# Transposing DMAs of gathered rows moved from ScalarE's queue to SyncE's, with a fourth buffer, new planned times, and expert 0's rows taken block by block

## The chip, the cores and the metric

The kernel runs on one core of one Trainium2 chip, as one launch. The metric is the device time of that launch in microseconds, the median of several executions. Profiles are of one execution; times in them are counted from the start of its span. Engines are named as the profile does: PE (TensorE), DVE (VectorE), ACT (ScalarE), POOL (GpSimd), SP (SyncE). A DMA is issued by an instruction on an engine's queue (SPq, ACTq, POOLq) and its data moves afterwards on the core's 16 DMA engines.

## The reference, cut to what matters

Three stages follow each other: a gated linear attention over 4 sequences, 8 heads, 768 steps, head size 48; a mixture of 8 experts, in which each of 3072 tokens goes to one expert; a second feed-forward layer over all tokens.

```python
# stage 1: state = alpha * state + k v^T ; y = q state
x = attn_out.transpose(0, 2, 1, 3).reshape(B * S, H * D)          # 3072 x 384
# stage 2
logits = unit(x) @ unit(expert_emb).T / tau
expert_idx = argmax(logits, axis=1)                                # one expert a token
for e in range(8):
    mask = expert_idx == e
    h = np.maximum(x[mask] @ w1[e], 0.0)                           # 384 -> 1024
    out[mask] = gate_w[mask, None] * (h @ w2[e])                   # 1024 -> 384
# stage 3
h = x @ w_in                                                       # 384 -> 2048
return np.maximum(0.01 * h, h) @ w_out                             # 2048 -> 384
```

## The kernel before, in words

**Precision.** Every matmul operand of stages 2 and 3 is a pair of float16 tiles, a high part and the rest; a product takes three matmuls (high by high, low by high, high by low). Making such a pair takes one instruction on ACT (the high part) and one on DVE (the rest).

**From stage 1 to stage 2.** Stage 1 ends with POOL scattering each token's row (384 values, a scale, a gate, the token's number, twice) into `bucket` in HBM, 3072 rows reserved for each expert (L596). Stage 2 reads for each expert the first 432 rows, in NB = 4 blocks of 128, 128, 128 and 48 rows.

**Stage 2, one expert.** `gather(e)` loads the 432 rows into one of two tiles `xg` (SP). `put_meta(e)` writes gate and token number of these rows back to HBM (two DMAs on SP, L841 and L843). For expert 0, `first_rows(n)` scales a block (DVE, L858), transposes it on PE (L854), and splits it into a pair (ACT L861, DVE L862). For experts 1 to 7, `block(e, n)` does this without PE: ACT writes the scaled high part and DVE the rest into one of three float16 buffers `xs16` (L874, L875), and one DMA transposes both into `xt`, of which there are two (L877). That DMA is issued on ACT's queue, behind the two instructions. `up(e, f)`, for f = 0 to 7, multiplies `w1` by `xt` into one of four PSUM banks (`ps1`; L932 to L934, nine matmuls of 432 columns); ACT and DVE empty the bank into `hh` and `hl` (L937, L938). `down(e, d)`, for d = 0 to 2, multiplies `w2` by these (L957 to L959, 24 matmuls of 432 columns), and ACT and DVE write the result into `x2h` and `x2l` (L963, L964). An expert is 144 matmuls of 432 columns.

**Weights beside it.** While expert e is computed, the eight pieces of expert e + 1's weights and four pieces of stage 3's weights are loaded into five stages `wstage` (`fetch`, SP, L886, 384 KB each) and converted into pairs by ACT and DVE (L891 and L892; L908 to L914 for the second layer's, which hold doubles).

**What sets the order.** All instructions of stage 2 are added to a `Plan` with an engine, a duration, what they read and write, and a wished time `at`. `Plan.order()` runs a list schedule: it takes the operation that can start first by the planned durations, and among those within 0.15 us of each other the one with the earliest `at`. A DMA has a `size`; it ends when a common channel of `rate` bytes per us has moved it, plus `land`. The resulting order is written out once: each engine's queue then works through its instructions in that order, and one that waits holds up all that are behind it on its queue, whatever the plan thought. In the plan the transposing DMA takes ACT 0.1 us, and lands 250e3 / 250e3 + 3.0 = 4.0 us later.

**Stage 3** runs over 3072 rows in six blocks of 512; PE does 288 x 3 matmuls of 512 columns and 384 x 3 of 384 columns (L774 to L794).

Of the kernel before, what the change touches and what calls it, by code (L numbers as in the profile page):

```python
# [10 lines left out]
F16 = mybir.dt.float16  # L11
# [10 lines left out]
P = 128  # L22
# [21 lines left out]
class Plan:  # L44
# [27 lines left out]
    def order(self):  # L72
        ops, n = self.ops, len(self.ops)
        after = [[] for _ in ops]
        for i, o in enumerate(ops):
            for d in o[3]:
                after[d].append(i)
        rank = [0.0] * n
        for i in reversed(range(n)):
            rank[i] = ops[i][1] + self.TAIL.get(ops[i][0], 0.0) + max((rank[j] + self.HOP for j in after[i]), default=0.0)  # L80
        left = [len(o[3]) for o in ops]
        free, end, start = {}, [0.0] * n, [0.0] * n
        wr, rd, port, chan = {}, {}, {"DVE": 0.0, "POOL": 0.0}, 0.0
        ready = [i for i in range(n) if not left[i]]
        done = []
        while ready:
            best = []
            for i in ready:
                eng, us, fn, deps, pe, ps, lock, at, size = ops[i]
                t = max([free.get(eng, 0.0)] + [end[d] + self.HOP if ops[d][0] != eng else start[d] + ops[d][1] for d in deps])  # L90
                t = max([t] + [rd.get(b, 0.0) + self.HOP for b in pe] + [wr.get(b, 0.0) + self.HOP for b in ps])
                if lock:
                    t = max(t, port["POOL" if eng == "DVE" else "DVE"])
                best.append((t, at, -rank[i], i))
            first = min(best)[0]
            t, _, _, i = min((b for b in best if b[0] <= first + 0.15), key=lambda b: b[1:])
            eng, us, fn, deps, pe, ps, lock, at, size = ops[i]
            start[i] = t
            free[eng] = t + us
            end[i] = t + us + self.TAIL.get(eng, 0.0)  # L100
            if size:
                chan = max(chan, t + us) + size / self.rate
                end[i] = chan + self.land
            for b in pe:
                wr[b] = max(wr.get(b, 0.0), end[i])
            for b in ps:
                rd[b] = max(rd.get(b, 0.0), end[i])
            if lock:
                port[eng] = max(port[eng], t + us)
            ready.remove(i)  # L110
            done.append(i)
            for j in after[i]:
                left[j] -= 1
                if not left[j]:
                    ready.append(j)
        assert len(done) == n
        self.start, self.end, self.done = start, end, done
        return sorted(done, key=lambda i: start[i])
# [51 lines left out]
def body(ctx, tc, qT, kT, aT, v, emb, tau, w1, w2, w_in, w_out, out):  # L170
# [99 lines left out]
    with tc.tile_pool(name="at", bufs=1) as rt, \  # L270
            tc.tile_pool(name="pa", bufs=1, space=PSUM) as pa:

        def tiles_of(name, shape, n=1, dtype=F32):
            return [rt.tile([P, *shape], dtype, name=f"{name}{i}", bufs=1) for i in range(n)]
# [2 lines left out]
        mask = tiles_of("mask", [P])[0]  # L277
        zero, none = tiles_of("zero", [AUG])[0], tiles_of("none", [X2 // P * 2 + 2])[0]
        ta, tq, tk = tiles_of("a", [AW], 3), tiles_of("q", [S], 3), tiles_of("k", [S], 3)
        tv, txb = tiles_of("v", [NC, D], 2), tiles_of("xb", [NC, AUG], 3)  # L280
        tbc, trc = tiles_of("bc", [AW], 2), tiles_of("rc", [AW], 3)
        tkh, tam = tiles_of("kh", [S], 2), tiles_of("am", [2, HC, P], 2)
        tkn, ten, tst = tiles_of("kn", [NC, 2, HD], 2), tiles_of("en", [HD, NC], 2), tiles_of("st", [HD, NC], 2)
# [7 lines left out]
        emb_sb = rt.tile([E, D], F32, name="emb_sb", bufs=1)  # L291
        ess = rt.tile([E, 8], F32, name="ess", bufs=1)
        emb_pad = rt.tile([E, H, 64], F32, name="emb_pad", bufs=1)

        psc = pa.tile([P, 2, 512], F32, name="psc")
        py = pa.tile([P, 2, 512], F32, name="py")
# [503 lines left out]
    with tc.tile_pool(name="mx", bufs=2) as mxp, tc.tile_pool(name="mh", bufs=1) as mhp, \  # L800
# [6 lines left out]
        xts = [mxp.tile([P, 2 * KD, CAP], F16, name=f"xt{i}", bufs=1) for i in range(2)]  # L807
        stages = first + [wst2.tile([P, CH], F32, name="wstage")]
        xrow = [mxp.tile([P, D], F32, name=f"xs{i}", bufs=1) for i in range(3)]
        xs16 = [mxp.tile([P, 2, D], F16, name=f"xs16{i}", bufs=1) for i in range(3)]  # L810
        hid = [[mhp.tile([P, CAP], F16, name=f"h{x}{f}") for f in range(NF1)] for x in "hl"]
        signs = [w64.tile([P, W64], F32, name=f"sg{i}") for i in range(2)]
        words = [w64.tile([P, W64], U32, name=f"t{i}") for i in range(2)]
# [1 line left out]
        ps2 = [pm.tile([P, CAP], F32, name=f"ps2{i}") for i in range(4)]  # L815
        size = [min(P, CAP - n * P) for n in range(NB)]
        NF = CAP // P
        plan = Plan(rate=250e3, land=3.0)
        V, S_, T_, Q_ = "DVE", "ACT", "PE", "SP"
        START, TURN = 20.0, 26.4  # L820

# [3 lines left out]
        def gather(e):  # L825
            xg = xgs[e % 2]

            def go():
                if e:
                    nc.sync.dma_start(xg[:, :NF], bucket[e * NT:e * NT + NF * P].rearrange("(n p) d -> p n d", p=P))  # L830
                for n in range(NF if e else 0, NB):
                    nc.sync.dma_start(xg[:size[n], n], bucket[e * NT + n * P:e * NT + n * P + size[n]])

            plan.add(Q_, 0.9 if e else 1.8, go, ["bucket"], [("xg", e % 2)], size=CAP * AUG * 4, at=begin(e - 2) + 8 if e > 1 else 20.0 * e)

        def put_meta(e):
            xg = xgs[e % 2]
# [9 lines left out]
        def first_rows(n):  # L847
            x, m = xrow[n % 3], size[n]
            xt, tp = xts[0], ps1[n][:, :KD * P].rearrange("p (k t) -> p k t", k=KD)
            hi, lo = xt[:, :KD, n * P:n * P + m], xt[:, KD:, n * P:n * P + m]  # L850

            def turn():
                for k in range(KD):
                    nc.tensor.transpose(tp[:, k, :m], x[:m, k * P:(k + 1) * P], ident[:m, :m])  # L854
                for _ in range(6 if n == NB - 1 else 2):
                    nc.tensor.matmul(ps2[3], ones16, busy[:, :CAP], start=True, stop=True)

            plan.add(V, 0.42, lambda: nc.vector.tensor_scalar(x[:m], xgs[0][:m, n, :D], xgs[0][:m, n, D:D + 1], None, op0=ALU.mult),  # L858
                     [("xg", 0)], [("row", n % 3)], at=n - 9.0)
            plan.add(T_, 0.5, turn, [("row", n % 3)], [("ps1", n)], at=n - 9.0)  # L860
            plan.add(S_, 0.47, lambda: nc.scalar.activation(hi, tp[:, :, :m], AF.Copy), [("ps1", n)], [("xt", 0, n, 0)], at=n - 9.0)  # L861
            plan.add(V, 0.56, lambda: nc.vector.scalar_tensor_tensor(lo, tp[:, :, :m], 1.0, hi, op0=ALU.mult, op1=ALU.subtract),  # L862
                     [("ps1", n), ("xt", 0, n, 0)], [("xt", 0, n, 1)], at=n - 9.0)
# [2 lines left out]

        def block(e, n):

            m, g = size[n], len(turned) % 3
            turned.append(n)  # L870
            x, r = xgs[e % 2][:m, n, :D], xgs[e % 2][:m, n, D:D + 1]
            xs, xt = xs16[g][:m], xts[e % 2]
            at = begin(e - 1) + 1.0 + 2.5 * n
            plan.add(S_, 0.62, lambda: nc.scalar.activation(xs[:, 0], x, AF.Copy, scale=r), [("xg", e % 2)], [("xs", g, 0)], at=at)  # L874
            plan.add(V, 0.61, lambda: nc.vector.scalar_tensor_tensor(xs[:, 1], x, r, xs[:, 0], op0=ALU.mult, op1=ALU.subtract),  # L875
                     [("xg", e % 2), ("xs", g, 0)], [("xs", g, 1)], at=at)
            plan.add(S_, 0.1, lambda: nc.scalar.dma_start_transpose(out=xt[:, :, n * P:n * P + m], in_=xs.rearrange("p i d -> p (i d)")),  # L877
                     [("xs", g, i) for i in range(2)], [("xt", e % 2, n, i) for i in range(2)], size=250e3, at=at + 2.0)

        fetched = []  # L880

# [83 lines left out]
                     [("ps2", b), ("x2", e, d), ("place", 1)], [("x2l", e, d)], at=at)  # L965

        with tc.manual_schedule():
            plan.add("WAIT", 10.0, lambda: None, [], ["bucket"])
            second = second_pieces()
            per = -(-len(second) // E)  # L970
            def pieces_of(e):
# [150 lines left out]
```

## Time and profile before

| | |
|---|---|
| median of 3 runs | 838.59 us (834.28 to 846.31) |
| the profiled execution, its own time | 838.9 us |
| its span | 837.2 us |
| mean granted clock of PE | 0.96 |
| PE busy | 771.9 us (92%), 5098 matmuls |
| DVE busy | 456.0 us (54%) |
| ACT busy | 338.5 us (40%) |
| POOL busy | 89.3 us (11%) |
| DMA | 84.07 MB, mean 100 GB/s |

The shares are means over three stages with different limits: stage 1 ends near 180 us, stage 2 runs to 454 us, stage 3 from there to the end. A matmul is pipelined, so its row shows a longer duration than the distance to the next one; the pace is read from the distance of start times. A row of a DMA instruction on a queue shows only how long the issue took; when the data has landed is told apart.

### The profile page before, as it was taken

To read this page: it belongs to the slowest core of one execution; us is meant where nothing else is said; L and a number is where in the kernel's file an instruction comes from. 1 tells how busy PE (TensorE), PEld (TensorE's weight loads), DVE (VectorE), ACT (ScalarE), POOL (GpSimd) and SP (SyncE) were. 2 spreads that over 40 slices of the span, in tenths; PEclk is the share of its full clock that TensorE was granted. 3 is DMA by queue.
4 is the path that set the end of the run, shared out by engine and by line. 5 is a ranking of instruction groups with operands and counts; after the bars stand their busy time and mean duration, and the time that the engine had idled before them with its cause. 6 is when DMAs were issued, how large, how long until landed. Compare 5 with 4: busy or idle time off the path is not lost.

```text
span 837.2 us, 12882 instructions
## 1 busy us (share of the span) xinstructions
PE 771.9 (92%) x5098; PEld 432.1 (52%) x5098; DVE 456.0 (54%) x784; ACT 338.5 (40%) x671; POOL 89.3 (11%) x92
## 2 busy tenths in 40 slices
PE   5999999887929598799999999999999999999996
PEld 3777767534515254355554455455455455455453
DVE  9989989544446677679853730620621621621610
ACT  1344536324344556567741521521521521522510
POOL 6122524220000000000000001001001001000000
PEclk8999999997969799899999999999999999999998
DMA  8874853337668696787700000000000000000000
GB/s 303 284 258 134 273 170 129 95 121 146 135 164 168 145 249 165 162 239 216 215 2 2 1 10 29 1 11 29 0 10 29 1 10 29 2 10 29 0 17 24
DMA packets 61665, 84.07 MB, mean 100 GB/s; under 512 B 29848, under 2 KB 40864, under 8 KB 61600
## 3 DMA queue, kind: packets, MB, share of 16 engines
q1 hardware_dynamic: 39424, 69.04, 29.1%
q10 hardware_dynamic: 19040, 4.65, 3.6%
q0 software_dynamic: 3136, 9.50, 2.9%
q8 instruction: 42, 0.69, 0.4%
q14 instruction: 23, 0.19, 0.1%
HBM read 66.80 MB, written 11.73 MB: 94 GB/s over the span
## 4 chain that ended last, share of the span: by engine, by line
issue 43%; PE 13%; DMA 7%; POOL 3%; DVE 2%; ACT 1%; ACTq 1%; POOLq 0%; DVEq 0%; SPq 0%
DMA xt<-xs 4%; POOL out L797 3%; PE ps L932 2%; PE ps L933 2%; PE ps L934 2%; PE ps L959 2%; PE ps L958 2%; PE ps L957 2%; DMA wstage<-in_w 1%; DMA wstage<-in_w_in 1%; DMA xg<-bucket 1%; DVE w1l L892 1%; DVE hl L938 0%; ACTq L877 0%; ACT w2h L891 0%
## 5 line engine op out<-in xcount | busy, mean ns | idle before, releaser
L780 DVE SCALAR_TENSOR_TENSOR g<-ps,r 128x512 f32<-128x512 f32 x96 | 65.7, 684 | 150.3 <-ACT r L779 150.3
L792 PE MATMUL ps<-woh,gh 128*128 128x384 f16 x384 | 125.2, 326 | 0.0
L793 PE MATMUL ps<-wol,gh 128*128 128x384 f16 x384 | 125.2, 326 | 0.0
L794 PE MATMUL ps<-woh,gl 128*128 128x384 f16 x384 | 125.2, 326 | 0.0
L774 PE MATMUL ps<-x2h,wih 128*128 128x512 f16 x288 | 109.2, 379 | 1.4 <-DVE x2l L964 1.4
L776 PE MATMUL ps<-x2h,wil 128*128 128x512 f16 x288 | 109.2, 379 | 0.0
L775 PE MATMUL ps<-x2l,wih 128*128 128x512 f16 x288 | 109.2, 379 | 0.0
L932 PE MATMUL ps<-xt,w1h 128*128 128x432 f16 x192 | 71.1, 370 | 37.6 <-DVE hl L938 37.6
L784 DVE TENSOR_TENSOR gl<-g,gh 128x512 f16<-128x512 f32 x96 | 66.5, 693 | 65.4 <-ACT gh L783 65.4
L783 ACT ACTIVATE gh<-g 128x512 f16<-128x512 f32 x96 | 60.4, 630 | 82.6 <-DVE g L780 82.5
L796 ACT ACTIVATE osb<-ps,ms 128x384 f32<-128x384 f32 x24 | 14.0, 582 | 159.4 <-PE ps L794 159.4
L933 PE MATMUL ps<-xt,w1h 128*128 128x432 f16 x192 | 71.1, 370 | 0.0
L934 PE MATMUL ps<-xt,w1l 128*128 128x432 f16 x192 | 70.6, 368 | 0.0
L957 PE MATMUL ps<-hh,w2h 128*128 128x432 f16 x192 | 66.4, 346 | 0.0
L958 PE MATMUL ps<-hl,w2h 128*128 128x432 f16 x192 | 66.4, 346 | 0.0
L959 PE MATMUL ps<-hh,w2l 128*128 128x432 f16 x192 | 66.4, 346 | 0.0
L797 POOL DMA_INDIRECT out<-osb,tki x24 | 23.7, 986 | 352.1 <-ACT osb L796 345.2
L779 ACT ACTIVATE r<-ps 128x512 f32<-128x512 f32 x96 | 56.0, 583 | 10.8 <-PE ps L776 10.8
L336 PE MATMUL pfill<-busy,ones 128*128 128x512 f16 x161 | 51.2, 416 | 1.5 <-POOL ident masks.py:199 1.5
L938 DVE SCALAR_TENSOR_TENSOR hl<-ps,hh 128x432 f16<-128x432 f32 x64 | 38.2, 603 | 23.0 <-ACT hh L937 22.9
L792 PEld LDWEIGHTS <-gh 128*128 128x128 f16 x384 | 37.6, 98 | 25.2
L793 PEld LDWEIGHTS <-gh 128*128 128x128 f16 x384 | 37.6, 98 | 25.1
(197 smaller groups left out, 1133.4 us busy)
## 6 DMA issues: line engine op xcount, KB each, us to landing
wstage<-in_w SPq DMA_DIRECT2D x64, 384.0 KB, 3.5
a<-in_aT SPq DMA_DIRECT2D x16, 387.5 KB, 4.1
k<-in_kT SPq DMA_DIRECT2D x16, 384.0 KB, 4.1
q<-in_qT SPq DMA_DIRECT2D x16, 384.0 KB, 7.1
wstage<-in_w_in SPq DMA_DIRECT2D x16, 384.0 KB, 6.7
wstage<-in_w_out SPq DMA_DIRECT2D x16, 384.0 KB, 4.0
v<-in_v SPq DMA_DIRECT2D x8, 576.0 KB, 8.0
xg<-bucket SPq DMA_DIRECT2D x7, 582.0 KB, 6.2
```

The costliest lines, as they stand in the source:

```text
L774: nc.tensor.matmul(ps, wih[:, k, fs], xh[:, k], start=k == 0, stop=False)
L775: nc.tensor.matmul(ps, wih[:, k, fs], xl[:, k], start=False, stop=False)
L776: nc.tensor.matmul(ps, wil[:, k, fs], xh[:, k], start=False, stop=k == KD - 1)
L792: nc.tensor.matmul(ps, ghs[f][:, ts], woh[:, f], start=f == 0, stop=False)
L793: nc.tensor.matmul(ps, ghs[f][:, ts], wol[:, f], start=False, stop=False)
L794: nc.tensor.matmul(ps, gls[f][:, ts], woh[:, f], start=False, stop=f == NF2 - 1)
L932: nc.tensor.matmul(ps, w1h[:, f, k], xt[:, k], start=k == 0, stop=False)
L933: nc.tensor.matmul(ps, w1h[:, f, k], xt[:, KD + k], start=False, stop=False)
L934: nc.tensor.matmul(ps, w1l[:, f, k], xt[:, k], start=False, stop=k == KD - 1)
L957: nc.tensor.matmul(ps, w2h[:, f, cols], hh, start=f == 0, stop=False)
L958: nc.tensor.matmul(ps, w2h[:, f, cols], hl, start=False, stop=False)
L959: nc.tensor.matmul(ps, w2l[:, f, cols], hh, start=False, stop=f == NF1 - 1)
```

## The change

It does five things in stage 2, and moves one group of tiles in stage 1.

- `block(e, n)`: the transposing DMA is issued by SP, no longer by ACT. In the plan it takes SP 1.25 us and lands 1.0 + 8.0 us after that. Its wished time is 1 us after its block's (it was 2), and the blocks of an expert are 4.0 us apart in their wished times (it was 2.5).
- The buffers `xs16` are four, no longer three, so that each block of an expert has its own.
- `gather(0)` is four planned operations, one for each block, each landing by itself (2.5 us after the channel), and `first_rows(n)` needs only its own block. The DMAs themselves are the same four.
- The plan's channel has 230e3 bytes per us (250e3), and 4.0 us to land (3.0); `bucket` is taken to be complete at 10.8 us of the plan (10.0).
- `txb`, the tiles that stage 1 scatters from, are allocated as the last of their pool.

```diff
@@ Plan.order
             if size:
+                size, land = size if isinstance(size, tuple) else (size, self.land)
                 chan = max(chan, t + us) + size / self.rate
-                end[i] = chan + self.land
+                end[i] = chan + land
...
-        tv, txb = tiles_of("v", [NC, D], 2), tiles_of("xb", [NC, AUG], 3)
+        tv = tiles_of("v", [NC, D], 2)
...
         emb_pad = rt.tile([E, H, 64], F32, name="emb_pad", bufs=1)
+        txb = tiles_of("xb", [NC, AUG], 3)
...
-        xs16 = [mxp.tile([P, 2, D], F16, name=f"xs16{i}", bufs=1) for i in range(3)]
+        xs16 = [mxp.tile([P, 2, D], F16, name=f"xs16{i}", bufs=1) for i in range(4)]
...
-        plan = Plan(rate=250e3, land=3.0)
+        plan = Plan(rate=230e3, land=4.0)
...
@@ gather(e)
-            def go():
-                if e:
-                    nc.sync.dma_start(xg[:, :NF], bucket[e * NT:e * NT + NF * P].rearrange("(n p) d -> p n d", p=P))
-                for n in range(NF if e else 0, NB):
-                    nc.sync.dma_start(xg[:size[n], n], bucket[e * NT + n * P:e * NT + n * P + size[n]])
-
-            plan.add(Q_, 0.9 if e else 1.8, go, ["bucket"], [("xg", e % 2)], size=CAP * AUG * 4, at=begin(e - 2) + 8 if e > 1 else 20.0 * e)
+            def block(n):
+                nc.sync.dma_start(xg[:size[n], n], bucket[e * NT + n * P:e * NT + n * P + size[n]])
+
+            def most():
+                nc.sync.dma_start(xg[:, :NF], bucket[e * NT:e * NT + NF * P].rearrange("(n p) d -> p n d", p=P))
+                for n in range(NF, NB):
+                    block(n)
+
+            if e == 0:
+                for n in range(NB):
+                    plan.add(Q_, 0.45, lambda n=n: block(n), ["bucket"], [("xg", 0), ("row", n)], size=(P * AUG * 4, 2.5), at=0.0)
+            else:
+                plan.add(Q_, 0.9, most, ["bucket"], [("xg", e % 2)] + ([("row", n) for n in range(NB)] if e == 2 else []), size=CAP * AUG * 4, at=begin(e - 2) + 8 if e > 1 else 20.0)
@@ first_rows(n)
-                     [("xg", 0)], [("row", n % 3)], at=n - 9.0)
-            plan.add(T_, 0.5, turn, [("row", n % 3)], [("ps1", n)], at=n - 9.0)
+                     [("row", n)], [("x", n % 3)], at=n - 9.0)
+            plan.add(T_, 0.5, turn, [("x", n % 3)], [("ps1", n)], at=n - 9.0)
@@ block(e, n)
-            m, g = size[n], len(turned) % 3
+            m, g = size[n], len(turned) % 4
...
-            at = begin(e - 1) + 1.0 + 2.5 * n
+            at = begin(e - 1) + 1.0 + 4.0 * n
...
-            plan.add(S_, 0.1, lambda: nc.scalar.dma_start_transpose(out=xt[:, :, n * P:n * P + m], in_=xs.rearrange("p i d -> p (i d)")),
-                     [("xs", g, i) for i in range(2)], [("xt", e % 2, n, i) for i in range(2)], size=250e3, at=at + 2.0)
+            plan.add(Q_, 1.25, lambda: nc.sync.dma_start_transpose(out=xt[:, :, n * P:n * P + m], in_=xs.rearrange("p i d -> p (i d)")),
+                     [("xs", g, i) for i in range(2)], [("xt", e % 2, n, i) for i in range(2)], size=(230e3, 8.0), at=at + 1.0)
...
-            plan.add("WAIT", 10.0, lambda: None, [], ["bucket"])
+            plan.add("WAIT", 10.8, lambda: None, [], ["bucket"])
```

## Rows read from the trace of the kernel before

**Rows 1.** Busy time by stretch: us, PE, PEld, DVE, ACT, POOL, clock, DMA share, GB/s.
```profile
194.00:358.00 164.00, 126.37 (x630) 64.68 (x629) 98.59 (x173) 82.66 (x155) 0.00 (x0) 0.86 0.74 172
380.00:406.00 26.00, 26.00 (x144) 13.97 (x143) 24.97 (x44) 19.78 (x36) 0.00 (x0) 1.00 0.85 246
406.00:454.00 48.00, 47.87 (x263) 25.54 (x261) 25.58 (x48) 20.76 (x41) 0.05 (x1) 1.00 0.17 50
454.00:837.00 383.00, 373.84 (x2016) 197.15 (x2015) 130.06 (x218) 122.91 (x217) 24.91 (x27) 0.99 0.04 13
```

**Rows 2.** The waits: engine and line, for whom: us in all, times, longest.
```profile
ACT xs L874 <- DMA xt<-xs: 52.1, 15, 9.0
...
PE ps L932 <- DVE hl L938: 37.6, 5, 15.7
```

**Rows 3.** Timeline of PE where it resumes: start, us, what, idle before.
```profile
250.04 0.52 PE L932 MATMUL ps<-xt,w1h 128*128 128x432 f16 x1 [15.72 <-DVE hl L938]
...
288.52 0.52 PE L932 MATMUL ps<-xt,w1h 128*128 128x432 f16 x1 [9.56 <-DVE hl L938]
...
352.92 0.52 PE L932 MATMUL ps<-xt,w1h 128*128 128x432 f16 x1 [4.64 <-DVE hl L938]
```

**Rows 4.** Timeline of ACT ahead of these: scaled blocks that waited for a buffer.
```profile
242.90 0.61 ACT L874 ACTIVATE xs<-xg 128x384 f16<-128x384 f32 x1 [4.96 <-DMA xt<-xs]
...
284.76 0.61 ACT L874 ACTIVATE xs<-xg 128x384 f16<-128x384 f32 x1 [6.95 <-DMA xt<-xs]
...
348.22 0.61 ACT L874 ACTIVATE xs<-xg 128x384 f16<-128x384 f32 x1 [6.80 <-DMA xt<-xs]
```

**Rows 5.** Timeline of PE: first and last of stage 2, and its two paces.
```profile
194.15 0.35 PE L932 MATMUL ps<-xt,w1h 128*128 128x432 f16 x1
...
214.44 0.35 PE L957 MATMUL ps<-hh,w2h 128*128 128x432 f16 x1
...
227.40 0.35 PE L959 MATMUL ps<-hh,w2l 128*128 128x432 f16 x1
...
289.19 0.57 PE L934 MATMUL ps<-xt,w1l 128*128 128x432 f16 x1
289.55 0.57 PE L932 MATMUL ps<-xt,w1h 128*128 128x432 f16 x1
...
453.52 0.35 PE L959 MATMUL ps<-hh,w2l 128*128 128x432 f16 x1
```

**Rows 6.** The transposing DMA's line: issue ns least, median, most; us to landing.
```profile
L877 ACTq DMA_TRANSPOSE xt<-xs x28: 1190/1238/3469, 194.1 to 399.4; - x28
...
DMA to landing us min/median/max: 4.5/6.9/9.3
```

**Rows 7.** Waits of SP's queue, columns as in rows 2.
```profile
SPq L886 <- DVE t L910: 45.3, 23, 4.2
SPq L886 <- DVE w2l L892: 35.7, 20, 5.2
SPq L843 <- DMA meta<-xg: 30.1, 8, 7.4
...
SPq L886 <- DVE w1l L892: 24.3, 17, 3.3
SPq L841 <- DMA xg<-bucket: 23.6, 6, 5.5
```

**Rows 8.** The fetches' line on SP, columns as in rows 6.
```profile
L886 SPq DMA_DIRECT2D wstage<-in_w x56: 327/328/593, 128.6 to 407.1; - x56
```

**Rows 9.** Timeline of ACT: a conversion that waited for its piece.
```profile
222.06 0.84 ACT L891 ACTIVATE w2h<-wstage 128x768 f16<-128x768 f32 x1 [4.50 <-DMA wstage<-in_w]
```

**Rows 10.** Timeline of the start of stage 2, all engines.
```profile
182.04 2.32 SPq L832 DMA_DIRECT2D xg<-bucket  x4
182.12 0.84 ACT L891 ACTIVATE w1h<-wstage 128x768 f16<-128x768 f32 x1 [11.18 <-DMA bucket<-xb,slot]
...
188.35 1.59 DVE L858 TENSOR_SCALAR xs<-xg 128x384 f32<-128x384 f32 x4
```

## The prediction, as it was put on record before the changed kernel ran

> **What bounds the kernel now.** I read the busy times by stretch first. In stage 3, from 454 us on, PE is busy 373.84 of 383 us at clock 0.99 [rows 1]; the change does not touch that. In stage 2 the reader is to see two regimes: from 194 to 358 us PE is busy 126.37 of 164 us at a mean clock of 0.86, from 380 to 454 us it has no gap and clock 1.00 [rows 1]. So the loss sits in the first five or so experts. The waits, read second, give it a size: PE's up matmuls were held five times, 37.6 us in all, each time until DVE had emptied a PSUM bank (`hl`) [rows 2, 3]. Third comes the question why `hl` was late, and ACT's own timeline answers it: shortly before each gap ended ACT stood still at a scaled block L874, until a transposing DMA had landed and given back its `xs16` buffer: 6.95 us until 284.76, with PE resuming at 288.52; 6.80 us until 348.22, with PE resuming at 352.92; the longest gap, 15.72 us, has 4.96 us until 242.90 and others before it [rows 3, 4]. In all ACT waited 52.1 us for this, 15 times [rows 2]. Behind the waiting L874, in queue order, stand the `hh` that would free the banks. PE can run four `up` steps ahead, then it stops.
>
> **The size of the loss.** PE's stage 2 runs from 194.15 to 453.52 plus one matmul, 259.6 us [rows 5]. At full pace, 71 steps take 227.40 - 214.44 = 12.96 us, 0.1825 us each [rows 5]; 8 experts x 144 matmuls x 0.1825 = 210.2 us. The loss is 49.4 us: 37.6 idle, and 11.8 in which PE ran after a gap at 0.36 us a matmul (289.19 to 289.55 [rows 5]), the lower of its two clock levels, 1.2 GHz, against 2.4. That is 2.4 us per gap.
>
> **The change, part by part.**
>
> *Four buffers.* A block then waits for the transpose of the same block one expert earlier, not for the third last. In the rows the waits are for transposes issued a few us before; one turn is 26.3 us (144 x 0.1825), and a transpose lands 4.5 to 9.3 us after issue [rows 6]. I take all 52.1 us of ACT's waits as gone, and with them the five gaps and their slow pace: -49.4. Bounds: none of it, if SP issues the transposes so late that the buffers are still held, and all of it.
>
> *The transposing DMA leaves ACT.* 28 issues of 1.238 us, 34.7 us, stop blocking ACT's queue (the longest took 3.469) [rows 6]. ACT's busy time was 82.66 of 164 us where the gaps were [rows 1], so by itself I cost this at nothing beyond the gaps counted above: it is the margin that lets ACT catch up.
>
> *The same DMA enters SP's queue.* Per turn SP issues 12 fetches at 0.328 us (3.9) [rows 8], a gather pair at 2.32 / 4 each (1.2) [rows 10], two meta writes, about as long as fetches (0.7), and waits (30.1 + 23.6) / 8 = 6.7 us between gather, first and second meta write [rows 7]: 12.5 us of 26.3. Four transposes add 5.0: 17.5. It fits, so no steady cost. But the new entry waits for DVE's rest of the block, and behind it stand fetches; ACT takes the pieces in order, and a late piece holds `hh` just as a buffer did. The nearest row for that is the conversion that waited 4.50 us for its piece [rows 9], after SP had worked through gathers and meta writes. Bounds: nothing, and one such stall in each of seven turns. I take one, in the first two turns, where the meta writes waited longest (7.4 us [rows 7], against a planned 1.2 for both together): 4.5 idle + 2.4 slow pace = +6.9.
>
> *Planned times.* Four us to land, 230e3 bytes per us, and 1.25 + 1.0 + 8.0 us for a transpose change only the order in which queues are written. The old plan gave a transpose 0.1 us of its engine and 4.0 to land, below the least landing measured, 4.5; the new one is near the most, 9.3 [rows 6]. I count it as what makes the other two terms come true, not as a term of its own. Wider wished times (4.0 apart) decide only between operations within 0.15 us: nothing. Landing on one queue with the fetches: I take the median 6.9, with 9.3 as upper bound, which is still inside the planned 10.25.
>
> *DMA and DVE.* A turn needs 12 x 0.393 MB of pieces and 432 x 388 x 4 = 0.67 MB of gathered rows, 5.4 MB; the stretch 380 to 406 moved 26.0 x 246 = 6.4 MB while PE had no gap [rows 1]. DVE was busy 24.97 of those 26.0 us [rows 1], partly overlapping records: it is what would be late next, and why I do not expect better than PE's pace.
>
> *Expert 0's rows one by one.* The gather starts at 182.04, all four blocks were scaled in one run from 188.35 to 189.9, and `up` began at 194.15 [rows 5, 10]. The blocks' trips through PE, ACT and DVE stood one behind another. If the first three are done when the last lands, `up` can begin some 1.5 us after its scaling (0.5 + 0.47 + 0.56, the plan's durations for transpose, copy and rest): 191.5 at best, -2.7; if DVE's order still puts the rows behind conversions, 0. I take -2, as the plan now lets block 0 go first. No price is shown for `txb`'s new place: ACT's first conversion waited 11.18 us for the scatters [rows 10], and if that wait went, conversions would run before the gather, off PE's path; if it stayed, nothing changes. I take 0, and 0 to -1 as bounds, since DVE could be clear sooner for the rows.
>
> **Sum**, against the profiled execution's 838.9 us (span 837.2; the median of the runs shown is 838.59, so no correction): 838.9 - 49.4 - 2 + 6.9 = 794.4.
>
> **The rivals.**
>
> (a) *Clean*: SP is never late. 838.9 - 49.4 - 2 = 787.5. For it: 17.5 of 26.3 us, and the gapless turn. Against: the plan gives `put_meta` 1.2 us, while its inner wait alone is 30.1 / 8 = 3.8 on average [rows 7].
>
> (b) *SP late in two to four turns*, or buffers still waited for in as many: 787.5 + 2 to 4 x 6.9 = 801 to 815. For it: SP also waited for free stages, 45.3 + 35.7 + 24.3 us [rows 7], so a transpose can stand behind a fetch that waits for DVE. Against: with ACT on time the stages come free on time.
>
> (c) *The wait changes its queue*: SP's issue time appears on the path, whole. Either 28 x 1.238 = 34.7 us, 787.5 + 34.7 = 822, or one stall in each of seven turns, 787.5 + 7 x 6.9 = 836. For it: every DMA but the scatters is then issued by one in-order queue. The Trainium skill, "Perfetto Trace Analysis", section "DMA Optimizations", says that where descriptor generation is the bottleneck, DMAs should be spread over the engines that can issue them; this change does the reverse. Were SP such a bottleneck here, that page would speak for this rival; the rows do not bear it out, with 12.5 us of issue and ordered waits in 26.3. The Trainium skill, "DMA: Bandwidth & Descriptors", section "Issuing engines are not separate DMA queues", says that spreading saves only sequencer time; by it the data moves no faster or slower, which no row shows yet.
>
> (d) *Slower: SP's turn gets longer than PE's.* Place: a transpose behind a fetch that waits for a stage, and the next fetches behind the transpose. If SP's waits for stages (105.3 / 8 = 13.2 us a turn [rows 7]) all stayed and added to the 17.5, a turn would be 30.7 us; with every issue at 3.469 us [rows 6], 39.6, and the time 787.5 + 7 x 13.3 = 881. It is slower by 2% from 855.4 on, 9.7 us over 26.3 in each of seven turns, that is from issues of 2.6 us on average. Against: the median issue is 1.238, and a stage wait is slack that a late SP uses up.
>
> **Chances.** The forecast (794) 0.35; (a) 0.22; (b) 0.22; (c) 0.14; (d) 0.07. About 2% either way is what a measurement of this kernel can tell from no change, since its runs spread from 834.28 to 846.31. Forecast, (a) and (b) lie below 821.8: faster 0.79. (c) is within 2%: 0.14. Slower: 0.07. The range takes (a) with its bounds on expert 0's start (2.7 and 1 instead of 2: 785.8) and (b): 785 to 815, which leaves 0.21 outside.
>
> **What would show it.** Right, if ACT's L874 no longer waits for `xt<-xs` (0 to 5 us in all), PE's wait at L932 for `hl` falls from 37.6 to under 8 us, the clock between 194 and 358 us rises from 0.86 to above 0.95, and stage 2's span on PE falls from 259.6 to about 217. The transposes then show on SPq with about 1.2 us an issue. (b) or (c) would show as waits of ACT's or DVE's conversions for `wstage`, or of PE for `xt`, and as SP waiting for DVE's L875. (d) would show as SP without slack. For expert 0, L858 should run in four separate pieces, and the first L932 come about 10 us after the gather's first issue, where it now comes 194.15 - 182.04 = 12.1 us after it. The forecast is wrong if a turn that has no buffer wait still has a gap of PE, or if stage 1 or stage 3 changes by more than 2 us.

## The result, and the profile after

The changed kernel took 810.84 us, median of 4 runs (809.85 to 810.95), the kernel before on the same chip 842.29 us (834.28 to 846.31): ratio 0.9635, 95% interval 0.9553 to 0.9718. The forecast was 794.4, the range 785 to 815. The time fell to rival (b), 801 to 815, not to the forecast. The profiled execution took 810.95 us with a span of 809.2.

Busy time by stretch of the changed kernel, columns as in [rows 1]:

```profile
194.00:358.00 164.00, 148.23 (x761) 76.64 (x759) 112.66 (x197) 95.75 (x180) 0.00 (x0) 0.93 0.74 187
380.00:406.00 26.00, 26.00 (x144) 13.95 (x143) 21.79 (x39) 18.75 (x34) 0.00 (x0) 1.00 0.66 201
...
427.00:809.00 382.00, 373.84 (x2016) 197.13 (x2015) 129.46 (x217) 122.39 (x216) 23.93 (x25) 1.00 0.04 13
```

In the stretch where PE was busy 126.37 us it is now busy 148.23, at clock 0.93 instead of 0.86: 164 - 148.23 = 15.8 us of gaps are left of 37.6. Stage 3 is unchanged, 373.84 us busy in both. PE's first and last matmul of stage 2, and the gaps between them (start, us, what, idle before):

```profile
190.01 0.35 PE L940 MATMUL ps<-xt,w1h 128*128 128x432 f16 x1
...
219.80 0.52 PE L940 MATMUL ps<-xt,w1h 128*128 128x432 f16 x1 [3.35 <-DMA xt<-xs]
...
236.46 0.52 PE L940 MATMUL ps<-xt,w1h 128*128 128x432 f16 x1 [7.01 <-DVE hl L946]
...
266.58 0.41 PE L940 MATMUL ps<-xt,w1h 128*128 128x432 f16 x1 [2.24 <-DVE hl L946]
...
279.28 0.34 PE L965 MATMUL ps<-hh,w2h 128*128 128x432 f16 x1 [1.55 <-ACT hh L945]
...
425.58 0.35 PE L967 MATMUL ps<-hh,w2l 128*128 128x432 f16 x1
```

Lines have moved: L874 is now L882, L877 is L885 (on SP), the fetch L886 is L894, the conversion L891 is L899, L932 is L940. PE's stage 2 lasts 425.58 + 0.18 - 190.01 = 235.75 us, where it was 259.6 [rows 5]: 23.85 us less. The spans differ by 28.0. The other 4 us lie ahead of stage 2: the first gather was issued at 177.79, before at 182.04 [rows 10], and there a wait of ACT in stage 1, 5.04 us in the kernel before, is missing from this execution (experiment e8):

```profile
162.01 0.49 ACT L458 ACTIVATE yT<-py 112x384 f32<-112x384 f32 x1 [5.04 <-remote]
```

The waits of the changed kernel's stage 2 (engine and line, for whom: us in all, times, longest):

```profile
ACT w1h L899 <- DMA wstage<-in_w: 18.1, 2, 9.3
...
ACT w2h L899 <- DMA wstage<-in_w: 11.7, 1, 11.7
...
PE ps L940 <- DVE hl L946: 9.2, 2, 7.0
...
ACT sg L916 <- DMA wstage<-in_w_in: 8.2, 3, 7.0
```

ACT's waits for pieces in the kernel before:

```profile
ACT w2h L891 <- DMA wstage<-in_w: 4.7, 2, 4.5
...
ACT sg L908 <- DMA wstage<-in_w_in: 1.1, 3, 0.5
```

The 52.1 us that ACT stood at scaled blocks [rows 2] are gone: L882 waits for `xt<-xs` nowhere. In their place ACT waits 40.1 us for weight pieces (38.0 in the three rows, 2.1 at `in_w_out`), a wait that came to 5.8 us before. Who was late with the pieces is told by SP's timeline ahead of the longest one, and ACT's row where it ends:

```profile
199.05 2.28 SPq L834 DMA_DIRECT2D xg<-bucket  x1
201.38 0.48 SPq L831 DMA_DIRECT2D xg<-bucket  x1
205.84 0.40 SPq L849 DMA_DIRECT2D meta<-xg  x1
209.53 0.34 SPq L851 DMA_DIRECT2D meta<-xg  x1
209.98 4.00 SPq L885 DMA_TRANSPOSE xt<-xs  x3
214.08 0.52 SPq L894 DMA_DIRECT2D wstage<-in_w  x1
```

```profile
217.42 0.84 ACT L899 ACTIVATE w2h<-wstage 128x768 f16<-128x768 f32 x1 [11.67 <-DMA wstage<-in_w]
```

From 201.86 to 209.98 SP issued two small writes and otherwise stood: `put_meta` waits for the gather just issued (L849), then for its own first write to land (L851). Three transposes stood behind it, and behind these the fetch that ACT was waiting for. PE's own wait of 3.35 us for `xt` at 219.80 has the same cause, and so has PE's longest gap, 7.01 us until 236.46. Ahead of it the next `put_meta` stood from 222.06 to 226.74, the fetches came behind it, and ACT got its piece at 233.27, and only then to the `hh` behind it:

```profile
221.65 0.41 SPq L849 DMA_DIRECT2D meta<-xg  x1
226.74 0.34 SPq L851 DMA_DIRECT2D meta<-xg  x1
227.20 0.35 SPq L894 DMA_DIRECT2D wstage<-in_w  x1
```

```profile
233.27 0.84 ACT L899 ACTIVATE w1h<-wstage 128x768 f16<-128x768 f32 x1 [9.31 <-DMA wstage<-in_w]
```

SP's waits at these two lines (before: [rows 7]):

```profile
SPq L851 <- DMA meta<-xg: 31.4, 8, 6.8
...
SPq L849 <- DMA xg<-bucket: 15.5, 5, 3.9
```

These were 30.1 and 23.6 us before, so the chain is old, and fetches stood behind it before, too. New are the transposes behind it, and that ACT, no longer held at its buffers, now comes to a piece before the piece has landed. The second alone is enough for the new wait: e5 below has it with no transpose on SP.

### The profile page after: what moved, and what is told of

Same layout as the page of the kernel before. It is cut to its first block, busy times and chain, and to the rows that moved or that the text cites. A ratio compares the mean times of both kernels' runs of the same rounds, so it can differ in the third digit from the quotient of the medians.

```text
span 809.2 us, 12898 instructions
## 1 busy us (share of the span) xinstructions
PE 769.7 (95%) x5098; PEld 431.5 (53%) x5098; DVE 455.8 (56%) x784; ACT 338.8 (42%) x671; POOL 89.3 (11%) x92
## 4 chain that ended last, share of the span: by engine, by line
issue 45%; PE 34%; DMA 7%; DVE 6%; POOL 4%; ACT 2%; SPq 1%; POOLq 0%; DVEq 0%; ACTq 0%
PE ps L966 3%; PE ps L967 3%; PE ps L965 3%; PE ps L942 3%; PE ps L941 3%; PE ps L940 3%; PE psc L398 3%; POOL out L799 3%; PE py L417 3%; PE py L449 2%; PE pfill L338 2%; DMA xg<-bucket 2%; DMA wstage<-in_w 2%; DMA meta<-xg 1%; PE ptr L477 1%
## 5 line engine op out<-in xcount | busy, mean ns | idle before, releaser
L940 PE MATMUL ps<-xt,w1h 128*128 128x432 f16 x192 | 69.0, 360 | 12.6 <-DVE hl L946 9.2
L941 PE MATMUL ps<-xt,w1h 128*128 128x432 f16 x192 | 69.0, 359 | 0.0
L942 PE MATMUL ps<-xt,w1l 128*128 128x432 f16 x192 | 68.7, 358 | 0.0
L799 POOL DMA_INDIRECT out<-osb,tki x24 | 23.6, 984 | 352.1 <-ACT osb L798 345.3
L781 ACT ACTIVATE r<-ps 128x512 f32<-128x512 f32 x96 | 55.9, 583 | 10.8 <-PE ps L778 7.9
L794 PEld LDWEIGHTS <-gh 128*128 128x128 f16 x384 | 37.6, 98 | 25.1
L795 PEld LDWEIGHTS <-gh 128*128 128x128 f16 x384 | 37.6, 98 | 25.1
L796 PEld LDWEIGHTS <-gl 128*128 128x128 f16 x384 | 37.6, 98 | 24.8
```

Of the source, the lines that this page charges most:

```text
L794: nc.tensor.matmul(ps, ghs[f][:, ts], woh[:, f], start=f == 0, stop=False)
L795: nc.tensor.matmul(ps, ghs[f][:, ts], wol[:, f], start=False, stop=False)
L796: nc.tensor.matmul(ps, gls[f][:, ts], woh[:, f], start=False, stop=f == NF2 - 1)
L940: nc.tensor.matmul(ps, w1h[:, f, k], xt[:, k], start=k == 0, stop=False)
L941: nc.tensor.matmul(ps, w1h[:, f, k], xt[:, KD + k], start=False, stop=False)
L942: nc.tensor.matmul(ps, w1l[:, f, k], xt[:, k], start=False, stop=k == KD - 1)
```

## The experiments

Three theories about the 24 to 27 us that stage 2 gained: the *buffer* (a fourth `xs16`), the *queue* (transposes off ACT), the *planned times*. And one about the 25.5 us of loss that stayed (235.75 - 210.2): `put_meta` on SP's queue. In e8, the changed kernel once more, the loss is 22.5 us, so differences of 3 us between single profiles say nothing.

| | what it is | us | ratio to before, 95% | PE's stage 2, us |
|---|---|---|---|---|
| | before | 835.3 to 842.3 | 1 | 259.6 |
| e1 | before, four buffers | 842.2 | 1.0016 to 1.0084 | 262.4 |
| e2 | before, transposes on SP | 822.5 | 0.9748 to 0.9832 | 243.9 |
| e5 | before, new planned times | 821.8 | 0.9745 to 0.9842 | 238.9 |
| e10 | before, `put_meta` on POOL | 833.4 | 0.9904 to 0.9997 | 257.7 |
| | changed | 810.8 | 0.9553 to 0.9718 | 235.8 |
| e6 | changed, old planned times | 828.6 | 0.9814 to 0.9913 | 247.5 |
| e3 | changed, three buffers | 813.0 | 0.9635 to 0.9713 | 232.0 |
| e7 | changed, one gather | 814.8 | 0.9662 to 0.9765 | 233.0 |
| e8 | changed, once more | 812.3 | 0.9630 to 0.9733 | 232.7 |
| e9 | changed, `put_meta` priced | 802.2 | 0.9574 to 0.9649 | 227.0 |
| e4 | changed, `put_meta` on POOL | 792.5 | 0.9393 to 0.9473 | 210.2 |
| e11 | e4, transposes on ACT | 788.0 | 0.9406 to 0.9505 | 210.2 |
| e12 | e4, old planned times | 791.0 | 0.9429 to 0.9533 | 213.4 |

The last column is from each one's profile, worked out as above. The kernels ran in three groups, e1 to e4, e5 to e8, e9 to e12, each beside the kernel before (839.2, 838.1 and 835.3 us); between groups the ratios are what compares.

**e1, the fourth buffer alone.**

```diff
-        xs16 = [mxp.tile([P, 2, D], F16, name=f"xs16{i}", bufs=1) for i in range(3)]
+        xs16 = [mxp.tile([P, 2, D], F16, name=f"xs16{i}", bufs=1) for i in range(4)]
...
-            m, g = size[n], len(turned) % 3
+            m, g = size[n], len(turned) % 4
```

> The kernel before with a fourth xs16 buffer and nothing else. If the loss was ACT waiting for a buffer (52.1 us of L874 waits, 37.6 us of PE gaps): the L874 waits fall below 10 us, PE's gaps below 20 us, and the time to about 815 us although the transposes stay on ACT's queue with the old planned times. If the queue or the planned times were what mattered: within 1% of the kernel before, 834 to 846 us.

842.2 us: nothing gained, and the theory behind my largest term fell. ACT's timeline of e1, experts 2 and 3 (blocks L874, transposes L877):

```profile
208.75 0.62 ACT L874 ACTIVATE xs<-xg 128x384 f16<-128x384 f32 x1 [1.16 <-DMA xg<-bucket]
...
213.63 0.61 ACT L874 ACTIVATE xs<-xg 48x384 f16<-48x384 f32 x1 [1.18 <-issue]
218.60 0.61 ACT L874 ACTIVATE xs<-xg 128x384 f16<-128x384 f32 x1 [4.36 <-DMA xg<-bucket]
218.66 1.23 ACTq L877 DMA_TRANSPOSE xt<-xs  x1
223.87 0.61 ACT L874 ACTIVATE xs<-xg 128x384 f16<-128x384 f32 x1 [4.65 <-DMA xt<-xs]
223.93 1.23 ACTq L877 DMA_TRANSPOSE xt<-xs  x1
232.28 0.61 ACT L874 ACTIVATE xs<-xg 128x384 f16<-128x384 f32 x1 [7.79 <-DMA xt<-xs]
```

Expert 3's blocks follow expert 2's after 9.85 us (208.75 to 218.60), not after a turn of 26.3. And each transpose is issued just before the block that needs its buffer: 218.66, then the block at 223.87; 223.93, then the block at 232.28. Later experts' blocks are 29.7 to 41.2 us apart (259.76, 297.41, 328.63, 358.31) and the four buffers are no help there either, since the transposes that free them still go out right ahead of the blocks:

```profile
323.16 1.23 ACTq L877 DMA_TRANSPOSE xt<-xs  x1
...
324.42 4.16 ACTq L877 DMA_TRANSPOSE xt<-xs  x3
328.63 0.61 ACT L874 ACTIVATE xs<-xg 128x384 f16<-128x384 f32 x1 [4.24 <-DMA xt<-xs]
```

The plan, which holds a transpose to be over after 4 us, ordered it so, and ACT stood as before: 35.0 us of waits for `xt<-xs`, 9 times.

**e2, the queue alone.**

```diff
-            plan.add(S_, 0.1, lambda: nc.scalar.dma_start_transpose(out=xt[:, :, n * P:n * P + m], in_=xs.rearrange("p i d -> p (i d)")),
+            plan.add(Q_, 0.1, lambda: nc.sync.dma_start_transpose(out=xt[:, :, n * P:n * P + m], in_=xs.rearrange("p i d -> p (i d)")),
```

> The kernel before with the transposing DMA on SP's queue and nothing else: three buffers, old planned times (0.1 us on its engine, 4 us to land). If buffers were the loss: ACT still waits for xt<-xs 40 us or more, and the time stays at 830 us or above, or rises, since the transposes are now planned as if they took SP 0.1 us and stand behind fetches that wait. If the 34.7 us of issue on ACT's queue was the loss: 810 to 820 us.

822.5 us, 17 less, between the two marks set (830 and 820). ACT still waited 17.1 us for buffers, and 29 us in three rows for pieces: the new wait is there from the queue alone.

**e3, the changed kernel with three buffers.**

```diff
-        xs16 = [mxp.tile([P, 2, D], F16, name=f"xs16{i}", bufs=1) for i in range(4)]
+        xs16 = [mxp.tile([P, 2, D], F16, name=f"xs16{i}", bufs=1) for i in range(3)]
...
-            m, g = size[n], len(turned) % 4
+            m, g = size[n], len(turned) % 3
```

> The changed kernel with three xs16 buffers again. If buffers were the loss: ACT waits for xt<-xs 30 us or more again and the time is 825 to 840 us. If queue and planned times carry the gain, and the planner can order three buffers as well as four: within 1% of the changed kernel's 810.8 us.

813.0 us, its interval inside that of the changed kernel (0.9553 to 0.9718); no block waits for a buffer. With e1: the fourth buffer is worth nothing in either kernel.

**e5, the planned times alone**, transposes still issued by ACT, three buffers.

```diff
...
-        plan = Plan(rate=250e3, land=3.0)
+        plan = Plan(rate=230e3, land=4.0)
...
-            plan.add(S_, 0.1, lambda: nc.scalar.dma_start_transpose(out=xt[:, :, n * P:n * P + m], in_=xs.rearrange("p i d -> p (i d)")),
-                     [("xs", g, i) for i in range(2)], [("xt", e % 2, n, i) for i in range(2)], size=250e3, at=at + 2.0)
+            plan.add(S_, 1.25, lambda: nc.scalar.dma_start_transpose(out=xt[:, :, n * P:n * P + m], in_=xs.rearrange("p i d -> p (i d)")),
+                     [("xs", g, i) for i in range(2)], [("xt", e % 2, n, i) for i in range(2)], size=(230e3, 8.0), at=at + 2.0)
```

> The kernel before with the planned times of the transposing DMA alone: 1.25 us of its engine, 8.0 us to land, 230e3 bytes per us, blocks still 2.5 us apart, three buffers, still issued on ACT. Theory 'times' (ACT waited for buffers because the plan took a transpose to be over after 4 us): ACT's waits of L874 (L875 here) for xt<-xs fall from 52 to under 10 us, and the time to about 815 (800 to 822). Rival 'queue' (what cost the time is the issue on ACT, 34.7 us, and its blocking of the conversions behind it): the waits may go, but the time stays at 830 or above. Third possibility, neither alone is enough: 822 to 830.

821.8 us, the upper end of what "times" allowed, well under the 830 of "queue". ACT's waits for buffers and for pieces (the scaled block is L875 here, the conversion L892):

```profile
ACT xs L875 <- DMA xt<-xs: 18.8, 8, 4.7
...
ACT w2h L892 <- DMA wstage<-in_w: 14.0, 4, 9.6
...
ACT sg L909 <- DMA wstage<-in_w_in: 8.1, 2, 8.0
ACT w1h L892 <- DMA wstage<-in_w: 6.7, 2, 4.6
```

The waits for buffers fell from 52.1 to 18.8 us, not under 10. So either the queue or the times give some 16 to 17 us alone. The new wait for pieces, 28.8 us in the three rows, is here too, with every transpose on ACT: SP wrote `put_meta`'s second part at 213.12, fetched at 213.59, and ACT stood 9.62 us for a piece until 220.08. The edit also gives every other DMA of the plan the new rate and landing, so the transposes' times are not told apart from those.

**e6, the changed kernel with the old planned times.**

```diff
-        plan = Plan(rate=230e3, land=4.0)
+        plan = Plan(rate=250e3, land=3.0)
...
-            at = begin(e - 1) + 1.0 + 4.0 * n
+            at = begin(e - 1) + 1.0 + 2.5 * n
...
-            plan.add(Q_, 1.25, lambda: nc.sync.dma_start_transpose(out=xt[:, :, n * P:n * P + m], in_=xs.rearrange("p i d -> p (i d)")),
-                     [("xs", g, i) for i in range(2)], [("xt", e % 2, n, i) for i in range(2)], size=(230e3, 8.0), at=at + 1.0)
+            plan.add(Q_, 0.1, lambda: nc.sync.dma_start_transpose(out=xt[:, :, n * P:n * P + m], in_=xs.rearrange("p i d -> p (i d)")),
+                     [("xs", g, i) for i in range(2)], [("xt", e % 2, n, i) for i in range(2)], size=250e3, at=at + 2.0)
```

> The changed kernel with the old planned times of the transpose (0.1 us of SP, 4.0 us to land by 250e3 and 3.0, 2.5 us apart); SP's queue, four buffers and expert 0's four gathers kept. Theory 'times count': about 822, as the kernel before with SP's queue alone gave (822.5), with ACT waiting over 10 us in all at the scaled blocks (L882) for xt<-xs or over 25 us for wstage. Rival 'the queue is all': 809 to 813, with these waits no larger than in the changed kernel.

828.6 us, 16 above e8 beside it and 6 above what "times count" expected: the times count in this kernel. In its stage 2 ACT waited 21.0 + 13.8 + 9.6 us for pieces and once 9.7 for a buffer.

**e4, `put_meta` off SP.**

```diff
-                so = nc.sync.value_load(offi[0:1, e:e + 1], min_val=0, max_val=NT)
-                nc.sync.dma_start(meta[ds(so, NF * P)].rearrange("(n p) c -> p n c", p=P), xg[:, :NF, D + 1:D + 3])
+                so = nc.gpsimd.value_load(offi[0:1, e:e + 1], min_val=0, max_val=NT)
+                nc.gpsimd.dma_start(meta[ds(so, NF * P)].rearrange("(n p) c -> p n c", p=P), xg[:, :NF, D + 1:D + 3])
...
-                    nc.sync.dma_start(meta[ds(so + NF * P, CAP % P)], xg[:CAP % P, NF, D + 1:D + 3])
+                    nc.gpsimd.dma_start(meta[ds(so + NF * P, CAP % P)], xg[:CAP % P, NF, D + 1:D + 3])
...
-            plan.add(Q_, 1.2, go, [("xg", e % 2)], [("meta", e)], at=begin(e) + 4)
+            plan.add("POOL", 1.2, go, [("xg", e % 2)], [("meta", e)], at=begin(e) + 4)
```

> The changed kernel with put_meta's two writes issued by POOL, which is idle in this stage, instead of SP. If the gaps that are left come from SP standing still between gather, first and second meta write (46.9 us of waits) while fetches stand behind: the waits of ACT's and DVE's conversions for wstage fall from 44 us to under 15, PE's gaps in stage 2 from 16 us to under 6, and the time to about 792 us. If they come from the DMA engines or from DVE being full: within 1% of 810.8 us.

792.5 us, some 20 below e3 beside it. The same stretch as above, and the waits for pieces that are left:

```profile
194.00:358.00 164.00, 164.00 (x897) 87.77 (x896) 131.07 (x227) 111.50 (x206) 9.68 (x15) 0.99 0.91 208
```

```profile
ACT w2h L899 <- DMA wstage<-in_w: 1.7, 2, 1.3
...
ACT w1h L899 <- DMA wstage<-in_w: 0.5, 2, 0.3
```

PE has no gap, and stage 2 lasts 210.24 us (196.43 to 406.49 + 0.18). The waits themselves are no shorter, only harmless: POOL stands for them (us in all, times, longest), and nothing of stage 2 is behind it.

```profile
POOL meta L851 <- DMA meta<-xg: 41.0, 7, 7.5
...
POOL meta L849 <- DMA xg<-bucket: 37.2, 2, 29.3
```

The edit also makes the plan write a new order. That this order and not SP's freedom closed the gaps is unlikely: e11 and e12 below have two other orders, and no gaps or 2.7 us.

**e9, `put_meta` on SP, but planned at about what it takes.** With SP's 31.4 us at L851, 8 times, and 0.74 us of issue it took 4.7 us on average, without its wait for the gather.

```diff
-            plan.add(Q_, 1.2, go, [("xg", e % 2)], [("meta", e)], at=begin(e) + 4)
+            plan.add(Q_, 5.5, go, [("xg", e % 2)], [("meta", e)], at=begin(e) + 4)
```

> The changed kernel with put_meta planned at 5.5 us of SP instead of 1.2, still on SP. Theory 'price' (the plan writes SP's transposes and fetches behind a step that it thinks over after 1.2 us): ACT's waits for wstage fall from about 38 us to under 15, stage 2 on PE from 235.8 us to under 222, the time to 793 to 801. Rival 'blocking' (SP really is held 5 to 6 us a turn, whatever the plan knows): PE still has gaps of 10 us or more in all, 805 to 813.

802.2 us, between the two theories. "Price" missed its three marks: the time is just above its 801, ACT waited 27.7 us for pieces instead of under 15, and stage 2 lasted 227.0 us instead of under 222. "Blocking" missed its two by less: PE's gaps are 9.5 us, not 10 or more, the time 2.8 us under its 805. By ratio, which is what compares between groups, e9 (0.9574 to 0.9649) is not told apart from e8 (0.9630 to 0.9733), and e4 lies clearly below both. In PE's stage 2 the right price took off 5.7 us against e8 and 8.8 against the changed kernel's first profile, a quarter to a third of the loss. The rest, 16.7 us down to e4's 210.2, went only when `put_meta` left SP, whose wait at L851 is still 30.9 us here.

**e10, `put_meta` on POOL in the kernel before**, same edit as e4.

> The kernel before with put_meta on POOL alone; transposes on ACT with the old planned times, three buffers. Theory 'SP's chain of waits matters once the transposes stand behind it': ACT still waits for xt<-xs 35 to 52 us in all and the time stays within 828 to 842. Rival 'SP was late before as well': 815 to 826, as much as the 20 us that the same edit gave on the changed kernel.

833.4 us. As the first theory had it the gain is small, and the interval ends just below 1; the waits grew past what I expected:

```profile
ACT xs L874 <- DMA xt<-xs: 65.0, 14, 7.1
...
PE ps L932 <- DVE hl L938: 29.2, 6, 10.2
```

A freed SP is worth some 20 us in the changed kernel and a few here, where ACT stands at its buffers.

**e11, e4 with the transposes issued by ACT again.**

```diff
-            plan.add(Q_, 1.25, lambda: nc.sync.dma_start_transpose(out=xt[:, :, n * P:n * P + m], in_=xs.rearrange("p i d -> p (i d)")),
+            plan.add(S_, 1.25, lambda: nc.scalar.dma_start_transpose(out=xt[:, :, n * P:n * P + m], in_=xs.rearrange("p i d -> p (i d)")),
```

> The changed kernel with put_meta on POOL (792.5 us) and its transposing DMAs issued by ACT again, planned 1.25 us there. Theory 'ACT's queue costs by itself' (28 issues of 1.24 us, 34.7 us, and each waits for DVE's rest): 800 to 815, with gaps of PE. Rival 'the queue is free once the plan knows the times and SP is clear of waits': 790 to 795, no gap of PE from 194 to 358 us.

788.0 us, no gap; the rival was right, its range of 790 to 795 a little high. The stretch from 194 to 358, and ACT's waits for buffers:

```profile
194.00:358.00 164.00, 164.00 (x901) 87.91 (x899) 134.97 (x233) 113.66 (x212) 9.08 (x14) 1.00 0.95 211
```

```profile
ACT xs L882 <- DMA xt<-xs: 0.2, 1, 0.2
```

**e12, e4 with the old planned times** (edit as in e6).

> The changed kernel with put_meta on POOL and the old planned times of the transpose (0.1 us of SP, 4 us to land). Theory 'times count by themselves' (16 us between the changed kernel with old and with new times): 803 to 812, PE gaps again. Rival 'they counted only beside a blocked SP': 790 to 796, no gaps.

791.0 us; again the rival. PE is left with 2.7 us of gaps in the stretch from 194 to 358, and the 8.2 us that ACT waited for buffers cost PE next to nothing. The ratios of e4, e11 and e12 cannot be told apart; all three beat both kernels. So once SP is clear, one of the two, queue or times, is enough, and it doesn't matter which. The fourth buffer was left in all three; whether it is needed there no run tells.

**e7, expert 0's gather as one planned operation**, `first_rows` waiting for all of it.

```diff
...
-            if e == 0:
-                for n in range(NB):
-                    plan.add(Q_, 0.45, lambda n=n: block(n), ["bucket"], [("xg", 0), ("row", n)], size=(P * AUG * 4, 2.5), at=0.0)
...
+            plan.add(Q_, 0.9 if e else 1.8, go, ["bucket"], [("xg", e % 2)], size=CAP * AUG * 4, at=begin(e - 2) + 8 if e > 1 else 20.0 * e)
...
-                     [("row", n)], [("x", n % 3)], at=n - 9.0)
+                     [("xg", 0)], [("x", n % 3)], at=n - 9.0)
```

> The changed kernel with expert 0's gather as one planned operation again, its blocks scaled only when all are there. Theory 'nothing gained by block' (first up matmul came 12.22 us after the gather's first issue, 12.11 before): within 2 us of the changed kernel, 809 to 813, first up matmul 12 to 13 us after the gather. Rival (the block by block start is worth what I counted, or more): 813 or above, and the first up matmul 14 us or more after the gather.

814.8 us, the rival's time (813 or above) but not its 14 us from gather to `up`; beside 812.3 for e8 it is a difference inside both intervals. The start of stage 2 in e7 (gather at 183.71, first `up` at 196.83) and in e8, which has the split (182.82 and 194.04):

```profile
190.64 0.88 PE L856 MATMUL ps<-ident,xs 128*128 128x128 f32 x3 [4.09 <-issue]
```

```profile
189.75 0.52 PE L862 MATMUL ps<-ident,xs 128*128 128x128 f32 x3 [2.40 <-issue]
```

e7 needs 13.1 us from gather to `up`, e8 11.2. But e9, which has the split, also needs 13.4, and its transposes ran at 0.88 us after an idle of 4.07, as in e7. Over all fourteen profiles the distance is 13.1 to 13.4 us where PE stood 4.1 to 4.3 us before its first transpose, and 11.2 to 12.3 where it stood 2.4 to 2.8; both occur with the split and without. What sets PE's idle time there, no run tells.

**e8, the changed kernel once more.**

> The changed kernel, unaltered, beside the three others: 809 to 813. It also tells whether stage 1's end moved because of the change: in the profile of the changed kernel the scatters of stage 1 ended about 4 us earlier than before, where a 5 us wait of ACT at L460 near 162 us was missing. Theory 'not the change': the wait is there again, the first gather is issued near 182 us, and the span is about 4 us longer than 809.2, with the time within 810 to 815. Rival (the place of txb took it away): no such wait, gather near 178 us, the time at 811 or below.

812.3 us. The span is 810.2, 1.0 longer than the changed kernel's first, not 4: stage 2 was 3.0 us shorter this time. Stage 1's wait is there again, as in the kernel before:

```profile
162.03 0.49 ACT L460 ACTIVATE yT<-py 112x384 f32<-112x384 f32 x1 [5.13 <-remote]
```

So the 4 us ahead of stage 2 in the changed kernel's profile are not the change's. Nor does the wait go with `txb`'s place: it is missing in e10, too, which has `txb` where it was before. What makes the wait come and go, no run tells.

## Why the prediction was right in its range and wrong in its steps

- **The size of the loss, 49.4 us, was right.** The gapless stage 2 of e4 and e11 lasts 210.24 us; 210.2 was worked out from PE's pace.
- **That the time fell into the range was in part luck.** The 49.4 us were credited to a part that was worth nothing, and came from two parts that were booked at nothing. The first profile's sum is 838.9 - 49.4 + 25.5 - 4.1 (stage 1) = 810.9, so stage 1's wait, which the change doesn't touch, moved it down as well.
- **"Four buffers: -49.4" is the step that failed.** I took the buffer that ACT waited for as what was short. It was not: three serve as well as four (e3), and four without the rest wait on (e1). The argument that a block then waits for a transpose of one expert earlier, with a turn of 26.3 us between, took that transpose to go out a turn ahead of the block. In e1 it goes out right ahead of it, whether the experts' blocks are 9.85 us apart or over a turn. What was short was the plan's 4 us for a transpose (e5, with the plan's other DMA times), on a queue with the conversions behind it. Its landing of 4.5 to 9.3 us [rows 6] rests on the seven of 28 that the trace has; e10, which issues them in the same way and has all 28, gives 2.4, 6.0 and 12.1 us (least, median, most).
- **"The transposing DMA leaves ACT: 0" and "Planned times: not a term of its own" were wrong.** Each takes 16 to 17 us off by itself (e2, e5). They cure the same wait, so together, with three buffers, they give 26 (e3), not 33; with SP clear, e11 does without the queue and e12 without the times.
- **"The same DMA enters SP's queue: +6.9" was mis-sized.** I named the mechanism (the wait at L849 and L851 before the transposes, fetches behind them, ACT held at a piece) and the point in the first turns, but priced one stall of 4.5 + 2.4. What stayed was 25.5 us, 15.8 of gaps and 9.7 of slow pace, 3.7 times that price (in e8 22.5, 18.4 and 4.1: the part at slow pace differs between executions). The working had counted 12.5 + 5.0 us of 26.3 and concluded that it fits: a mean share of a queue says nothing about who stands behind its longest wait. e4 shows that all of this loss goes with `put_meta`'s place, and e5 that it is the fetches behind `put_meta`, with or without transposes between.
- **The rivals.** (a) warned that the plan gives `put_meta` 1.2 us against 3.8 for its inner wait; e9 shows that this misprice is a quarter to a third of the loss in stage 2, if that much. (b) came true, by SP being late, not by its alternative of buffers still waited for. (c) and (d) did not: SP's waits for free stages at L894 still hold 20.3 + 19.9 + 13.1 us of slack. The Trainium skill, "DMA: Bandwidth & Descriptors", section "Issuing engines are not separate DMA queues", says that issuing from several engines saves only sequencer time; e4 and e11, equal within their intervals with the transposes on SP or on ACT, agree. What cost time here was not issuing but waiting in order: SP's two writes, 0.40 and 0.34 us of issue, held it for 8 us. The Trainium skill, "Perfetto Trace Analysis", section "DMA Optimizations", says that it may make sense, above all with loops or control flow, to give inputs one issuing engine and outputs another. e4 does that for `meta`, without a loop, and its 20 us agree.
- **Expert 0's rows: -2 became 0** (12.22 us from gather to `up`, 12.11 before; e7). **DMA, DVE and `txb` at 0** held: in e11 DVE is busy 134.97 of 164 us and PE has no gap.
- **The signs.** Two signs of being wrong came true: a turn without a buffer wait still had gaps of PE (7.01 us until 236.46), and stage 1 moved by more than 2 us. L874's wait went to 0, as forecast. PE's wait for `hl` fell to 9.2 (below 8 was forecast), the clock rose to 0.93, and 0.96 in e8 (above 0.95), stage 2 shrank to 235.75 (217). L858's four pieces appear as three (two blocks ran together). But a limit of 2 us on stage 1 was finer than that stage repeats itself: it moved by 5 us between the two profiles of the changed kernel (gathers at 177.79 and 182.82).

## What to carry to other kernels

When an engine waits for a buffer, look at when the DMA that frees it was issued and what the plan believes of its duration, before adding a buffer: here the list schedule, with a too short landing, put the transpose that frees the buffer right ahead of the block that needs it, and a fourth buffer did not change that. Before DMAs are moved to another queue, list that queue's own waits by place, since whatever is put behind a wait inherits it whole, however low the queue's mean use; a small write that waits on another belongs on a queue with nothing behind it. Undo the parts one at a time: here the costly part was one that the change had not touched.

## What the runs showed of the hardware that had not been expected

A transpose's issue took 1.23 to 1.31 us in the median of every run, on SP or ACT, but single ones took up to 1.92 us (e10) to 4.50 (e5), and four in a row took 8.23 us in e4, 2.06 each. And landing was not one number. In runs whose traces have all 28 of them, least, median and most were 2.7, 5.1 and 9.1 us in the changed kernel and 2.6, 5.2 and 8.3 in e9, with SP issuing; with ACT issuing 2.4, 6.0 and 12.1 in e10, and in e11:

```profile
L885 ACTq DMA_TRANSPOSE xt<-xs x28: 1192/1232/2702, 192.0 to 351.9; - x28
...
DMA to landing us min/median/max: 2.8/7.8/14.5
```

The DMA engines were busy 0.74 of the stretch from 194 to 358 us before and after the change, 0.89 in e12, 0.91 in e4 and 0.95 in e11. Whether the issuing queue or what moves beside a transpose makes the difference, no run separates; e11 lost no time by it.
